# Zero-padded inverses in one place, weight splits one block ahead, and later reloads in a gated mix of linear attention and ReGLU

## The chip, the core and the metric

The kernel runs on one core of a Trainium2 chip. The metric is the device time of one execution in microseconds; the time before is the median of three runs. One further execution was taken by the hardware profiler, and all durations below come from it.

## The reference

```
g = sigmoid((x * gate_w).sum(-1))                       # x: 2048 x 576
q, k, v = split(x @ wqkv)                               # 32 heads of 18
phi(t) = concat(softmax(t @ w_phi), softmax(-t @ w_phi))  # per head
kv = sum_s phi(k)^T v ;  z = sum_s phi(k)
o = phi(q) kv / (phi(q) z + 1e-6)
a = o @ wo
b = (relu(x @ W_gate) * (x @ W_up)) @ W_down            # 576 -> 4608 -> 576
out = g * a + (1 - g) * b
```

All data are float32. The products are made in float32r with operands split into a high and a low part; the FFN's products go by a seven-product block scheme.

## The kernel before

**Stages.** The values of the first 512 tokens come first (L217 to L237): warm-up matmuls, then loads of a slice of x and of wv for each of five row groups k, split into high and low by ScalarE (ACT) and VectorE (DVE). A loop over tokens then makes keys, values, queries and the running sum kv. The out-projection goes over four blocks of 512 tokens, b = 0 to 3 (in the order BLOCKS). The FFN follows in two halves of 36 units, with a swap of operands and accumulators between the halves.

**The out-projection of one block.** `sums(b, ...)` (L556) multiplies the features ph with kvm, which gives numerators and denominators together. ACT copies the result to R and og (L560), and SP's queue gathers the denominators into dn (L562, L564). `invert(b)` takes the reciprocal on VectorE (L593), multiplies it with the gate (L594) and stores the product on SP into rows of kt (L595). `split_inverse(b)` splits it on POOL into rd, high and low (L603, L604); rd has two halves of 64 rows, one for odd and one for even b. `divide(b, k)` spreads the inverses of row group k over 128 rows by a matmul of rd with 0/1 columns (L616), multiplies R by them on VectorE (L618), and makes oh on ACT (L619) and ol on VectorE (L620). `first_out(k, mm)` (L633, block 0) or `project_out(b, m)` (L175, blocks 1 to 3) multiplies oh and ol with the output weights wo. `rows_out` copies the result o (L769 to L772) and stores it to att on SP (L773). `fetch` (L431) loads the features of a block from DRAM on POOL's queue, after `store_turned` (L392) has stored the last of them. Denominators and numerators share PSUM banks called kv, po and pw.

**What sets the order.** A scheduler orders ACT and VectorE; `in_order` keeps TensorE, SP and POOL in the order of the code, `after` and `behind` hold named instructions behind others. An instruction that waits holds all that stands behind it on its engine or queue.

**FFN.** `load_w(u)` loads the raw weights wr of unit u, and `unit(u)` splits them to wb, makes block sums of wr and splits these to ws (L846 to L870). The x operands xo are partly made in place from loaded rows: high part on ACT (L829, L830), low part on VectorE (L834, L814); `early()` does this for the operands 5 and 6. `step(u, j)` makes one of the seven products (L1098) of a unit, with ACT's copies g and u (L1259), VectorE's sums (L1378 to L1383, L1255) and down products (L1138, L1161) whose results are added to accumulators ac. wdr is the raw down weight of a unit, loaded on SP (L1031) and split to wd by ACT (L1061) and VectorE (L1064). At the swap `add_up` stores finished accumulators (L1182) and loads those of the second half from att (L1106); split weights of the first half come back from DRAM as wb and ws (L883, L884).

Of the kernel before, what the change touches and what calls it, by code (L numbers as in the profile page):

```python
# [14 lines left out]
DH = D // H  # L15
P = 128
# [67 lines left out]
def gated_mix_kernel(  # L84
# [126 lines left out]
    with tc.tile_pool(name="ps_v", bufs=1, space=PSUM) as ps_v:  # L211
# [7 lines left out]
        for k in range(5):  # L219
            w = raw.tile([P, TB + VW], F32, name="xwv", tag="raw")  # L220
            nc.sync.dma_start(w[:, :TB], xT[:, k, :TB])
            nc.sync.dma_start(w[:, TB:], wv[:, k])
# [367 lines left out]
    def invert(b):  # L590

        dn = DN.pop(b)
        nc.vector.reciprocal(dn, dn)  # L593
        tt(out=dn, in0=gT[:, BLOCKS[b] * P:(BLOCKS[b] + 1) * P], in1=dn, op=MULT)  # L594
        nc.sync.dma_start(kt_[2 * H * (b % 2):][:H, :TB], dn)  # L595

    def split_inverse(b):

        if not RD:
            RD.append(rb.tile([4 * H, TB], F32R, name="rd", bufs=1))  # L600
        i = 2 * H * (b % 2)
        d2, hi, lo = kt_[i:i + H, :TB], RD[0][i:i + H], RD[0][i + H:i + 2 * H]
        nc.gpsimd.tensor_copy(hi, d2)  # L603
        pt(out=lo, in0=d2, in1=hi.bitcast(F32), op=SUB)  # L604

    def divide(b, k):

        R = RW[b]
        n = P if k < 4 else 64
        if k == 4:  # L610
            pool = op_ if b else rb
            OW[b] = [pool.tile([P, j, TB], F32R, name=f"o{a}", bufs=2 if b else 1) for a, j in (("h", 5), ("l", 4))]
        oh, ol = OW[b]
        ps = kv_bank(1 - k % 2 if b > 1 or b == 1 and k < 2 else 0)
        half = slice(2 * H * (b % 2), 2 * H * (b % 2 + 1))
        nc.tensor.matmul(ps[:n], spread[half, k, :n], RD[0][half], start=True, stop=True)  # L616
        r = R[:n, k]
        tt(out=r, in0=ps[:n], in1=r, op=MULT)  # L618
        nc.scalar.activation(oh[:n, k], r, AF.Copy)  # L619
        tt(out=ol[:, k] if k < 4 else oh[64:, k], in0=r, in1=oh[:n, k].bitcast(F32), op=SUB)  # L620
# [43 lines left out]
    with in_order(tc, nc, nc.tensor, nc.sync, nc.gpsimd):  # L664
# [67 lines left out]
        divide(0, 3)  # L732
        two = pp.tile([P, 2, TB], F32, name="pw", tag="pp")
# [195 lines left out]
    with in_order(tc, nc, nc.tensor, nc.sync, nc.gpsimd):  # L929
        x0, x1, x2 = (operand_ahead(i) for i in range(3))  # L930
        fetch(BLOCKS[3], nc.gpsimd)
        load_operand(0, 0, nc.gpsimd)
        load_operand(0, 1, nc.gpsimd)
        first_out(2, range(5))
        halves = two[:, 0], two[:, 1]
        sums(2, (4, 5), halves)
        divide(0, 0)
        first_out(1, range(5))
        sums(2, (3, 2), halves)
# [5 lines left out]
        sums(2, (1, 0), halves)  # L945
        gather(2, 4)
        invert(2)
        gather(2, 3, 2, 1, 0)
        split_inverse(2)
        divide(1, 1)  # L950
        divide(1, 0)
        for m in range(5):
# [4 lines left out]
            if m == 2:  # L957
                gather(3, 4)
                invert(3)
                gather(3, 3, 2, 1, 0)  # L960
                split_inverse(3)
                whole(x0)
            if m > 0:
                divide(2, 5 - m)
            if m in (0, 1):
                root_rows(m + 2)
            if m == 4:
                divide(2, 0)
                whole(x1)
# [272 lines left out]

    def add_up():

        if PEND:
            done.extend(PEND.pop()())
        store(done)
        done.clear()
# [38 lines left out]
    def step(u, j):  # L1287
# [122 lines left out]
        if u == 0:  # L1410
            if j < 3:
                next(early, None)
            elif j < 5:
# [30 lines left out]
    later_half, early = second_half(), early()  # L1444
# [93 lines left out]
def _layout(A_x, A_wqkv, A_w_phi, A_wo, B_W_gate, B_W_up, B_W_down, gate_w):  # L1538
# [33 lines left out]
    spread = np.zeros((4, H, 5, P), np.float32)  # L1572
    for r in range(QK):
# [4 lines left out]
    for k in range(5):  # L1578
        for r in range(P):
            spread[:, wo_rows[k * P + r] // DH, k, r] = 1.0  # L1580
# [20 lines left out]
```

## Time and profile before

| | |
|---|---|
| median of three runs | 1607.55 us (1607.47 to 1607.68) |
| the profiled execution | 1607.92 us |
| its span, first to last instruction | 1605.9 us |
| mean granted TensorE clock | 0.997 |
| HBM read, written | 172.67 MB, 109.21 MB |
| TensorE matmuls | 7823 |

The span is what the trace shows; the execution's time holds some 2 us around it. A row of the timeline gives the start in us from the span's start, the duration in us, engine, line, operation, the tile written and read, shapes, and how often; a bracket gives the idle time of the engine just before the row and what ended it. A row of the waits names the engine that waited, the tile and line, what released it, the total, the number of times and the longest. PEld is TensorE's weight load, which runs beside its matmuls.

### The profile page before, as it was taken

Reading aid. Unit: us, or ns where it says so; the run is one execution under the profiler, and the core shown is the slowest. Engines: PE = TensorE matmul, PEld = TensorE weight load, DVE = VectorE, ACT = ScalarE, POOL = GpSimd, SP = SyncE. Lnnn points to the kernel's source line nnn. Section 1 sums busy time; section 2 is a strip of 40 time slices with the busy share of each in tenths; the row PEclk is TensorE's granted clock in tenths of the full one; section 3 lists DMA queues with packets and bytes.
Section 4 is the critical chain, followed back from the end, with each engine's and each line's share of the span. In section 5 each row is a group of like instructions: output and inputs, shape, how many; then the busy total and the mean of one; then the engine's idle time right before and its main releaser. Section 6 shows DMA issues by size and latency. Waiting matters only on the chain.

```text
span 1605.9 us, 20175 instructions
## 1 busy us (share of the span) xinstructions
PE 1580.5 (98%) x7823; PEld 1314.5 (82%) x7823; DVE 1192.4 (74%) x1864; ACT 559.9 (35%) x918; POOL 171.3 (11%) x234
## 2 busy tenths in 40 slices
PE   9999999899999999999999999999999999999998
PEld 9899995577888888888888887788888888888887
DVE  4997775477787877878777777677776777767777
ACT  4444335463332332333333234223223232232331
POOL 0125522100000000000000002111111111111110
PEclk9999999999999999999999999999999999999999
DMA  5373415569655565655554525634344343443432
GB/s 165 108 242 134 162 41 148 177 234 351 215 220 212 217 249 217 222 218 189 214 197 172 208 83 175 242 129 183 134 151 181 129 174 143 148 184 129 169 148 74
DMA packets 65370, 284.59 MB, mean 177 GB/s; under 512 B 6842, under 2 KB 17338, under 8 KB 56572
## 3 DMA queue, kind: packets, MB, share of 16 engines
q1 hardware_dynamic: 62828, 273.30, 46.8%
q0 software_dynamic: 1872, 8.97, 1.8%
q8 instruction: 61, 1.00, 0.2%
q10 hardware_dynamic: 576, 1.05, 0.2%
q14 instruction: 33, 0.27, 0.0%
HBM read 172.67 MB, written 109.21 MB: 176 GB/s over the span
## 4 chain that ended last, share of the span: by engine, by line
PE 91%; DMA 3%; DVE 3%; ACT 1%; issue 1%; POOL 0%; SPq 0%; ACTq 0%; DVEq 0%; POOLq 0%
PE cx L1098 28%; PE ca L1098 13%; PE pd L1138 12%; PE pd L1161 10%; PE cy L1098 7%; PE kv L175 4%; PE pq L175 3%; PE pk L175 3%; PE pm L1138 2%; PE pm L1161 2%; PE kv L417 1%; DMA dn<-R 1%; PE ptr L374 1%; PE pv L237 1%; DMA wdr<-wd 1%; PE pw L175 1%
## 5 line engine op out<-in xcount | busy, mean ns | idle before, releaser
L1205 ACT ACTIVATE hh<-g 128x512 fp32r<-128x512 f32 x195 | 120.1, 624 | 459.1 <-DVE g L1255 289.8
L1176 DVE TENSOR_TENSOR ac<-pd,ac 128x512 f32<-128x512 f32 x238 | 164.0, 689 | 145.9 <-PE pd L1161 145.7
L1098 PE MATMUL cx<-xo,wb 128*128 128x512 f32 x1008 | 250.9, 392 | 5.0 <-DVE u L1380 3.5
L1098 PE MATMUL cx<-xo,ws 128*128 128x512 f32 x1008 | 252.4, 390 | 3.0 <-ACT g L1259 2.8
L1098 PE MATMUL ca<-xo,ws 128*128 128x512 f32 x1008 | 252.0, 389 | 0.6 <-DMA ws<-wsd 0.6
L1098 PEld LDWEIGHTS cx<-xo,wb 128*128 128x128 f32 x1008 | 189.2, 189 | 47.1 <-DVE u L1380 4.4
L1098 PEld LDWEIGHTS cx<-xo,ws 128*128 128x128 f32 x1008 | 188.9, 188 | 43.8 <-ACT g L1259 4.7
L1098 PEld LDWEIGHTS ca<-xo,ws 128*128 128x128 f32 x1008 | 189.1, 188 | 40.3 <-issue 1.0
L1138 PE MATMUL pd<-hh,wd 128*128 128x512 f32 x576 | 200.7, 389 | 0.0
L1161 PE MATMUL pd<-hh,wd 128*128 128x512 f32 x476 | 185.2, 389 | 0.0
L1144 DVE TENSOR_TENSOR ac<-pd,ac 128x512 f32<-128x512 f32 x144 | 99.1, 688 | 106.6 <-PE pd L1138 103.1
L1210 DVE TENSOR_TENSOR hl<-g,hh 128x512 fp32r<-128x512 f32 x195 | 136.4, 699 | 1.9 <-ACT hh L1205 0.2
L1259 ACT ACTIVATE g<-cx 128x512 f32<-128x512 f32 x144 | 84.9, 590 | 128.1 <-PE cx L1098 128.0
L1138 PEld LDWEIGHTS pd<-hh,wd 128*128 128x128 f32 x576 | 108.1, 188 | 22.6
L1098 PE MATMUL cy<-xo,wb 128*128 128x512 f32 x504 | 125.9, 389 | 0.0
L1061 ACT ACTIVATE wd<-wdr 128x384 fp32r<-128x384 f32 (+1 forms) x106 | 62.3, 606 | 152.9 <-DMA wdr<-wd 152.9
L1138 PE MATMUL pd<-hl,wd 128*128 128x512 f32 x288 | 112.2, 389 | 1.0 <-ACT xo L830 1.0
L1098 PEld LDWEIGHTS cy<-xo,wb 128*128 128x128 f32 x504 | 94.6, 188 | 19.6
L1161 PEld LDWEIGHTS pd<-hh,wd 128*128 128x128 f32 x476 | 89.4, 188 | 18.5
L1161 PE MATMUL pd<-hl,wd 128*128 128x512 f32 x238 | 92.6, 389 | 0.0
L814 POOL TENSOR_TENSOR xo<-xr,xo 32x512 fp32r<-32x512 f32 x5 | 8.2, 1637 | 653.9 <-DVE xo L814 646.1
L1064 DVE TENSOR_TENSOR wd<-wdr,wd 128x384 fp32r<-128x384 f32 (+1 forms) x106 | 69.3, 669 | 5.5 <-ACT wd L1061 5.5
(250 smaller groups left out, 2564.9 us busy)
## 6 DMA issues: line engine op xcount, KB each, us to landing
wsd<-ws SPq DMA_DIRECT2D x34, 1280.0 KB
ws<-wsd SPq DMA_DIRECT2D x34, 1280.0 KB
wbd<-wb SPq DMA_DIRECT2D x34, 960.0 KB
wb<-wbd SPq DMA_DIRECT2D x34, 960.0 KB
wr<-wgu SPq DMA_DIRECT2D x36, 768.0 KB
wdr<-wd SPq DMA_DIRECT2D x36, 576.0 KB
eT<-et SPq DMA_DIRECT2D x10, 594.0 KB
xt<-xb SPq DMA_DIRECT2D x7, 768.0 KB
```

What stands on the lines that cost most here:

```text
L175: nc.tensor.matmul(ps, w, m, start=i == 0, stop=i == len(pairs) - 1)
L237: nc.tensor.matmul(pv[i][c], m, w_[:, k, cs], start=k == 0 and n == 0, stop=k == 4 and n == 1)
L1061: nc.scalar.activation(o[:, 0], a, AF.Copy)
L1064: tt(out=o[:, 1], in0=a, in1=o[:, 0].bitcast(F32), op=SUB)
L1098: nc.tensor.matmul(ps, w, v, start=first and m == 0, stop=m == len(pairs) - 1, skip_group_check=True)
L1138: nc.tensor.matmul(ps, w, v, start=k == 0 and (i < 2 or first), stop=k == len(mms) - 1 and (i < 2 or last), skip_group_check=True)
L1144: tt(out=a, in0=ps, in1=a, op=ADD)
L1161: mm = lambda ps, w, v, a, z: nc.tensor.matmul(ps, w, v, start=a, stop=z, skip_group_check=True)
L1176: tt(out=a, in0=ps, in1=a, op=ADD)
L1205: nc.scalar.activation(h, src, AF.Copy)
L1210: tt(out=l, in0=src, in1=h.bitcast(F32), op=SUB)
L1259: nc.scalar.activation(a, ps, AF.Copy)
```

## The change

It has five parts. The first two wv loads are issued from ACT's queue. The inverses of all blocks lie in one place: rd keeps 64 rows of data and 64 rows of zeros, and L616 multiplies all 128 rows. The out-projection is written in another order: where invert and split_inverse stand, which sums come ahead of first_out, and where POOL's loads stand. The first two units' weight splits come one block of the out-projection earlier, and early() moves from the first FFN unit to the last block. At the swap a reload comes three calls of add_up after its store, and load_rests one step earlier.

```diff
-            nc.sync.dma_start(w[:, TB:], wv[:, k])
+            (nc.scalar if k < 2 else nc.sync).dma_start(w[:, TB:], wv[:, k])
...
-        nc.sync.dma_start(kt_[2 * H * (b % 2):][:H, :TB], dn)
+        nc.sync.dma_start(kt_[:H, :TB], dn)
...
             RD.append(rb.tile([4 * H, TB], F32R, name="rd", bufs=1))
-        i = 2 * H * (b % 2)
-        d2, hi, lo = kt_[i:i + H, :TB], RD[0][i:i + H], RD[0][i + H:i + 2 * H]
+            nc.gpsimd.memset(RD[0][2 * H:].bitcast(F32), 0.0)
+        d2, hi, lo = kt_[:H, :TB], RD[0][:H], RD[0][H:2 * H]
...
-        half = slice(2 * H * (b % 2), 2 * H * (b % 2 + 1))
-        nc.tensor.matmul(ps[:n], spread[half, k, :n], RD[0][half], start=True, stop=True)
+        nc.tensor.matmul(ps, spread[:, k], RD[0], start=True, stop=True)
...
         divide(0, 3)
+        quotients = last_of(nc, nc.vector)
...
         divide(0, 2)
         gather(1, 4)
-        with after(tc, nc, nc.vector, last_of(nc, nc.vector)):
+        with after(tc, nc, nc.vector, quotients):
             invert(1)
         gather(1, 3, 2, 1, 0)
-        split_inverse(1)
...
         fetch(BLOCKS[3], nc.gpsimd)
-        load_operand(0, 0, nc.gpsimd)
-        load_operand(0, 1, nc.gpsimd)
-        first_out(2, range(5))
+        first_out(2, range(3))
         halves = two[:, 0], two[:, 1]
         sums(2, (4, 5), halves)
+        first_out(2, range(3, 5))
         divide(0, 0)
+        split_inverse(1)
+        sums(2, (3, 2), halves)
         first_out(1, range(5))
-        sums(2, (3, 2), halves)
+        sums(2, (1, 0), halves)
+        gather(2, 4)
         for m in range(5):
             first_out(0, (m,))
             rows_out(0, m, PW[m])
             if m in (0, 1, 3):
                 divide(1, (4, 3, None, 2)[m])
-        sums(2, (1, 0), halves)
-        gather(2, 4)
-        invert(2)
-        gather(2, 3, 2, 1, 0)
-        split_inverse(2)
+            if m == 3:
+                with after(tc, nc, nc.vector, last_of(nc, nc.vector)):
+                    invert(2)
+                gather(2, 3, 2, 1, 0)
         divide(1, 1)
         divide(1, 0)
+        split_inverse(2)
+        load_operand(0, 0, nc.gpsimd)
+        load_operand(0, 1, nc.gpsimd)
         for m in range(5):
             project_out(1, m)
...
             if m == 2:
                 gather(3, 4)
-                invert(3)
-                gather(3, 3, 2, 1, 0)
-                split_inverse(3)
                 whole(x0)
             if m > 0:
                 divide(2, 5 - m)
+            if m == 3:
+                with after(tc, nc, nc.vector, last_of(nc, nc.vector)):
+                    invert(3)
+                gather(3, 3, 2, 1, 0)
...
             if m == 4:
                 divide(2, 0)
+                split_inverse(3)
                 whole(x1)
         for m in range(5):
             project_out(2, m)
...
-        unit0, unit1 = unit(0), unit(1)
+            if m > 1:
+                with behind():
+                    if m == 2:
+                        unit0, unit1 = unit(0), unit(1)
+                        next(unit0)
+                    if m == 3:
+                        whole(unit0)
+                    if m == 4:
+                        next(unit1)
+        first = early()
         for m in range(5):
             project_out(3, m)
             with behind():
                 if m == 0:
-                    next(unit0)
-                if m == 1:
-                    whole(unit0)
-                if m == 2:
-                    next(unit1)
+                    whole(unit1)
                 if m == 3:
-                    whole(unit1)
+                    next(first)
+                if m == 4:
+                    next(first)
...
     def store(keys):
         for hf, i, m, t in keys:
             nc.sync.dma_start(out[rows(i, m, t, hf)], ACC.pop((hf, i, m, t)))
-            if hf == 0:
-                load_acc(1, i, m, t)
...
-            if i in (3, 4):
-                load_rests(1, (2, 3, 4) if i == 3 else (5, 6))
+            if i in (2, 3):
+                load_rests(1, (2, 3, 4) if i == 2 else (5, 6))
...
     def add_up():
 
+        if len(STORED) > 2:
+            for hf, i, m, t in STORED.pop(0):
+                if hf == 0:
+                    load_acc(1, i, m, t)
         if PEND:
             done.extend(PEND.pop()())
         store(done)
+        STORED.append(tuple(done))
         done.clear()
...
         if u == 0:
-            if j < 3:
-                next(early, None)
-            elif j < 5:
+            if 3 <= j < 5:
                 plain_down(0, (high, low)[j - 3])
```

The 0/1 columns are filled for the first 64 rows only. Three places show how the order moves; line numbers of the changed kernel are one lower here than those before, up to 17 higher in the FFN.

VectorE around the reciprocal of block 1 (L593). The ol rows are, from the top, those of block 0's row groups k = 3 and 2; before:

```order
L620 TENSOR_TENSOR ol<-R,oh 128x512
L618 TENSOR_TENSOR R<-kv_2978,R 128x512
L313 TENSOR_TENSOR gates<-gates 128x8
L314 TENSOR_SCALAR gates<-gates 128x8
L620 TENSOR_TENSOR ol<-R,oh 128x512
L593 RECIPROCAL dn<-dn 128x128
L594 TENSOR_TENSOR dn<-kt,dn 128x128
L618 TENSOR_TENSOR R<-kv_3032,R 128x512
```

And in the changed kernel:

```order
L619 TENSOR_TENSOR ol<-R,oh 128x512
L617 TENSOR_TENSOR R<-kv_2979,R 128x512
L593 RECIPROCAL dn<-dn 128x128
L619 TENSOR_TENSOR ol<-R,oh 128x512
L594 TENSOR_TENSOR dn<-kt,dn 128x128
L313 TENSOR_TENSOR gates<-gates 128x8
L314 TENSOR_SCALAR gates<-gates 128x8
L617 TENSOR_TENSOR R<-kv_3031,R 128x512
```

The reciprocal of block 1 moved from behind the ol of k = 2 to ahead of it.

TensorE at the end of first_out(2). kv_2967 before and kv_2968 after are the bank of output rows m = 3, kv_3094 and kv_3089 the divide of k = 0; L556 is sums(2, ...). Before:

```order
L633 MATMUL kv_2967<-oh,wo 128x512
L633 MATMUL kv_2967<-ol,wo 128x512
L633 MATMUL kv_2967<-oh,wo 128x512
L633 MATMUL pw<-oh,wo 128x512
L633 MATMUL pw<-ol,wo 128x512
L556 MATMUL po<-ph,kvm 64x512 x3
L616 MATMUL kv_3094<-rd,spread 128x512
L633 MATMUL pw<-oh,wo 128x512
```

And in the changed kernel:

```order
L556 MATMUL po<-ph,kvm 64x512 x3
L632 MATMUL kv_2968<-oh,wo 128x512
L632 MATMUL kv_2968<-ol,wo 128x512
L632 MATMUL kv_2968<-oh,wo 128x512
L632 MATMUL pw<-oh,wo 128x512
L632 MATMUL pw<-ol,wo 128x512
L615 MATMUL kv_3089<-rd,spread 128x512
L556 MATMUL po<-ph,kvm 64x512 x4
L632 MATMUL pw<-oh,wo 128x512
```

The first pair of sums moved ahead of the last two m of first_out(2), and the second pair (the x4 row) from behind first_out(1) to directly behind the divide of k = 0.

VectorE at the end of block 3. wb and ws are the split weights of unit 1, xo the in-place operands, o the last 64 output rows of block 3. Before:

```order
L867 TENSOR_TENSOR wr<-wr 128x384
L772 TENSOR_TENSOR o<-o,kv_3634 64x512
L868 TENSOR_TENSOR wr<-wr 128x384
L834 TENSOR_TENSOR xo<-xo 128x1024
L869 TENSOR_TENSOR wr<-wr 128x384
L814 TENSOR_TENSOR xo<-xr,xo 32x512
L870 TENSOR_TENSOR wr<-wr 128x384
```

And in the changed kernel:

```order
L869 TENSOR_TENSOR wr<-wr 128x384
L848 TENSOR_TENSOR ws<-wr,ws 128x4x256
L851 TENSOR_TENSOR ws<-wr,ws 32x4x128
L833 TENSOR_TENSOR xo<-xo 128x1024
L813 TENSOR_TENSOR xo<-xr,xo 32x512
L833 TENSOR_TENSOR xo<-xo 128x1024
L813 TENSOR_TENSOR xo<-xr,xo 32x512
L833 TENSOR_TENSOR xo<-xo 128x1024
L813 TENSOR_TENSOR xo<-xr,xo 32x512
L771 TENSOR_TENSOR o<-o,kv_3639 64x512
L833 TENSOR_TENSOR xo<-xo 128x1024
L813 TENSOR_TENSOR xo<-xr,xo 32x512
```

The last add of block 3 moved from between the block sums of unit 1 to behind both weight splits and three of the four operands.

More of the change, by code (lines that the diff above doesn't have):

```diff
@@ L1241, in gated_mix_kernel @@
     done = []
+    STORED = []
     def add_up():
+        if len(STORED) > 2:
+            for hf, i, m, t in STORED.pop(0):
+                if hf == 0:
+                    load_acc(1, i, m, t)
         if PEND:
@@ L1442, in step @@
                 load_operand(1, 1)
-    later_half, early = second_half(), early()
+    later_half = second_half()
     with in_order(tc, nc, nc.tensor, nc.vector, nc.scalar, nc.gpsimd, nc.sync):
@@ L1572, in _layout @@
     spread = np.zeros((4, H, 5, P), np.float32)
+    copies = spread[:2]
     for r in range(QK):
@@ L1579, in _layout @@
         for r in range(P):
-            spread[:, wo_rows[k * P + r] // DH, k, r] = 1.0
+            copies[:, wo_rows[k * P + r] // DH, k, r] = 1.0
     spread = spread.reshape(4 * H, 5, P)
```

## The prediction

> **What bounds the kernel now.** I read the page first, then TensorE's waits over the whole span, then busy time by stage. The page: TensorE is busy almost throughout.
>
> ```profile
> PE 1580.5 (98%) x7823; PEld 1314.5 (82%) x7823; DVE 1192.4 (74%) x1864; ACT 559.9 (35%) x918; POOL 171.3 (11%) x234
> ```
>
> 1605.9 - 1580.5 leaves 25.4 us of idle TensorE, so an edit that removes no matmul can win only a piece of that, plus time lost to a slow clock or to slow steps between matmuls. Where the idle time lies:
>
> ```profile
> PE cx L1098 <- DVE u L1380: 3.5, 2, 2.9
> PE cx L1098 <- ACT g L1259: 2.8, 3, 1.3
> PE kv L616 <- POOL rd L604: 2.6, 1, 2.6
> PE pv L217 <- DVE warm L215: 1.5, 1, 1.5
> PE cx L1098 <- DMA wb<-wbd: 1.4, 1, 1.4
> PE po L556 <- issue: 1.1, 1, 1.1
> ```
>
> The columns are total, times, longest. By stage (length; busy PE, PEld, DVE, ACT, POOL; granted clock):
>
> ```profile
> 340.00:367.00 27.00, 23.23 (x100) 18.25 (x99) 21.63 (x29) 16.52 (x22) 0.00 (x0) 1.00 0.83 295
> 367.00:405.00 38.00, 37.21 (x155) 30.27 (x156) 26.97 (x41) 14.37 (x20) 0.00 (x0) 0.96 0.88 331
> 405.00:960.00 555.00, 555.00 (x2450) 459.57 (x2449) 433.82 (x654) 188.05 (x253) 0.00 (x0) 1.00 0.55 203
> 960.00:1050.00 90.00, 85.00 (x370) 68.59 (x369) 62.04 (x91) 31.55 (x55) 15.04 (x19) 1.00 0.53 186
> ```
>
> From 405 to 960 there is nothing to win. The change touches the start, the out-projection (about 256 to 346), the FFN's start (340 to 372) and the swap of halves (960 to 1050). Two short stretches run at half clock:
>
> ```profile
> 303.60:307.00 3.40, 3.40 (x10) 2.58 (x11) 1.22 (x2) 1.11 (x2) 0.99 (x2) 0.50 0.68 243
> 368.45:371.85 3.40, 3.40 (x9) 2.65 (x8) 2.29 (x5) 2.31 (x3) 0.00 (x0) 0.50 1.03 433
> ```
>
> Each follows a TensorE wait of 2.6 or 2.9 us (the L616 and L1380 rows above), and 3.4 us at half clock do the work of 1.7. So a stall of that size really costs 1.7 us more. The Trainium skill, "TensorE: Matmul & The Clock Gate", Part 1, says the clock falls after an idle window of about 3.4 us in a free-running grid. The trace differs in one point: 2.6 us sufficed. By the page's rule taken strictly, only the longest wait below (4.2 us) could lose the clock at all, and the sum would be 1.7 us lower.
>
> **The start.** Lines L221/L222: the first two wv loads go to ACT's queue.
>
> ```profile
> 1.65 0.43 SPq L222 DMA_DIRECT2D xwv<-wv  x1
> ```
> ```profile
> 5.73 0.69 ACT L148 ACTIVATE wv_h<-xwv 128x588 fp32r<-128x588 f32 x1 [1.26 <-DMA xwv<-wv]
> ```
> ```profile
> 1.46 4.04 PE L217 MATMUL pv<-warm 128*128 128x294 f32 x15 [1.46 <-DVE warm L215]
> 6.48 1.84 PE L237 MATMUL pv<-wv_h,xh 128*128 128x294 f32 x6 [0.98 <-ACT wv_h L148]
> ```
>
> The first real matmul waits 0.98 us for ACT's split, which waits for wv's landing. The load can be issued up to about 0.9 us sooner, and the warm-up matmuls end at 1.46 + 4.04 = 5.50, so 0.98 is the most that this wait can give. ACT's own queue now holds two issues ahead of its first copy, but ACT idles 1.26 us there already. Taken: **-0.9** (ends 0 and -2.7: the upper end adds one grid step of 1.7, if TensorE without a gap gets its full clock sooner). The Trainium skill, "DMA: Bandwidth & Descriptors", section "Issuing engines are not separate DMA queues", says that another queue saves issue time alone; by it this would be one issue, 0.43 us.
>
> **Spread matmuls over 128 rows.** L616 runs 20 times.
>
> ```profile
> L616 PE MATMUL kv<-rd,spread x20: 388/498/684, 258.0 to 329.2; 64*128 64x512 f32 x16, 64*64 64x512 f32 x4
> ```
> ```profile
> 268.73 0.50 PE L616 MATMUL kv<-rd,spread 64*128 64x512 f32 x1
> 269.16 0.50 PE L633 MATMUL pw<-oh,wo 128*128 128x512 f32 x1
> 269.50 0.40 PE L633 MATMUL pw<-ol,wo 128*128 128x512 f32 x1
> 269.73 0.62 PE L633 MATMUL pw<-oh,wo 128*128 128x512 f32 x2
> ```
>
> The normal pace is the last step, 0.23. The steps 268.73 to 269.16 and on to 269.50 are 0.43 and 0.34, so a 64-row tile costs 0.31 beside its own time; 20 times 0.31 is 6.2. Many stand next to waits, or to L556's own 108*64 tiles, which stay. I count 8: **-2.5** (0 to -4). The zero rows are one POOL memset before the first reciprocals arrive, so nothing waits for it.
>
> **Block 0's third quotient behind block 1's reciprocal.** VectorE before:
>
> ```profile
> 265.60 0.69 DVE L620 TENSOR_TENSOR ol<-R,oh 128x512 fp32r<-128x512 f32 x1 [0.42 <-ACT oh L619]
> 271.96 0.95 DVE L593 RECIPROCAL dn<-dn 128x128 f32<-128x128 f32 x1 [5.66 <-DMA dn<-R]
> 272.95 0.29 DVE L594 TENSOR_TENSOR dn<-kt,dn 128x128 f32<-128x128 f32 x1
> ```
>
> That first row is ol for k=2; first_out(2) read it at 269.50. In the changed order the RECIPROCAL stands ahead of it, and it waits 5.66 us for the dn loads, which nothing in the change makes earlier (POOL's four ph fetches still run beside them). So ol starts where the dn product started, 272.95, ends at 273.64, and TensorE, which cannot pass it, goes on at about 273.7: **+4.2** (3.2 to 5). Behind it queue dn's product, the gates and R for k=1, which TensorE needs later only.
>
> **sums(2,(3,2)) behind divide(0,0).** Before, first_out(1) lay between.
>
> ```profile
> 276.52 1.51 DVE L620 TENSOR_TENSOR ol<-R,oh 128x512 fp32r<-128x512 f32 x1 [0.70 <-ACT oh L619]
> ```
> ```profile
> 278.07 0.59 ACT L560 ACTIVATE R<-po 64x512 f32<-64x512 f32 x1 [1.58 <-DVE ol L620]
> ```
> ```profile
> 278.71 1.94 PE L556 MATMUL po<-ph,kvm 108*64 108x512 f32 x8 [0.19 <-ACT R L560]
> ```
>
> The ol is k=0's. The copy that empties the second po half writes R of block 2, in block 0's old buffer, so it waits for the last ol of block 0, and the sums that reuse that half wait for the copy. The chain R (0.7), oh (0.7), ol (0.7 to 1.5), copy (0.6) starts one matmul after divide(0,0), and with 14 matmuls of 0.23 between, 0.19 us was left to wait. Now only the two matmuls of the first half (0.9) cover it: 2.9 to 3.7 less 0.9 is 2.0 to 2.8. Taken: **+2.5** (1.5 to 3.1).
>
> **What goes.** The 2.58 us at block 2's first divide:
>
> ```profile
> 303.56 0.68 PE L616 MATMUL kv<-rd,spread 64*64 64x512 f32 x1 [2.58 <-POOL rd L604]
> ```
>
> All of sums(2) now precedes first_out(0), and SP issues its dn loads before block 0's first four att stores, so that chain starts 14 matmuls (3.2 us) and four issues sooner: **-2.6** (0 to -2.6). What is late next is block 2's VectorE queue, below. POOL's fetch and store of the last block stood behind the split of block 1:
>
> ```profile
> 275.52 0.60 POOL L603 CAST rd<-kt 32x512 fp32r<-32x512 f32 x1 [14.66 <-DMA kt<-dn]
> 276.21 1.28 POOL L604 TENSOR_TENSOR rd<-kt,rd 32x512 fp32r<-32x512 f32 x1
> 277.44 0.58 POOL L392 DMA_DIRECT2D eT<-et  x1
> 278.01 1.65 POOL L431 DMA_DIRECT2D ph<-eT  x3
> ```
>
> They now go some microseconds sooner, so the 1.1 us "issue" idle at an L556, which I take for a late ph, may go: **-0.5** (0 to -1.1). They then lie beside kt<-dn of block 1, whose 2.3 us (end of L594 at 273.24 to 275.52) may become 5 to 8, under first_out(1) and two pairs of sums, which hide it. The xr loads now follow block 2's split; no wait on them stands in the list.
>
> **Clock.** The half-clock step after 303.56 goes (-1.7); the waits of 4.2 and 2.5 us bring one each (+3.4): **+1.7** (-1.7 to +3.4).
>
> **Blocks 2 and 3.**
>
> ```profile
> 297.89 0.95 DVE L593 RECIPROCAL dn<-dn 128x128 f32<-128x128 f32 x1 [6.49 <-DMA R<-og]
> ```
>
> RECIPROCAL and product of block 2 (0.95 + 0.29) now stand among the last two quotients of block 1, ahead of project_out(1,0), which cannot start without them: **+1.3** (0 to 2.5). Block 3's inversion waits for divide(2,2), its split for divide(2,0), since there is one place: 0.95 + 0.29 + 2.3 + 0.6 + 1.3 = 5.4 from reciprocal to divide(3,4), under project_out(1,4) and project_out(2,0), 14 matmuls or 3.2 us each: **+1.0** (0 to 3).
>
> **FFN start.** The weight splits come earlier, the in-place operands 5 and 6 later, on a VectorE that is busy 21.63 of 27 us.
>
> ```profile
> 343.29 0.96 DVE L849 TENSOR_TENSOR wb<-wr,wb 128x768 fp32r<-128x768 f32 x1 [3.50 <-ACT wb L846]
> ```
> ```profile
> 354.69 0.67 DVE L772 TENSOR_TENSOR o<-o,kv 64x512 f32<-64x512 f32 x1
> ```
> ```profile
> 362.56 1.23 DVE L834 TENSOR_TENSOR xo<-xo 128x1024 fp32r<-128x1024 f32 x1
> ```
> ```profile
> 360.72 1.26 ACT L1061 ACTIVATE wd<-wdr 128x1024 fp32r<-128x1024 f32 x2
> ```
>
> The L772 add now stands behind both weight splits and three operands, just ahead of the last operand, the 362.56 row: 7.9 us later in its queue. Its att store stands ahead of the first wdr load on SP, that load ahead of ACT's wd (6.0 us from the add to it), and VectorE's wd ahead of the u of L1380. Against it, the first split (343.29) has 3.5 us of idle VectorE in front of it and may start that much sooner, and TensorE comes 4.2 us later (the terms above added up). I take these to cancel, **0** (-4.6, the 2.9 us wait and its clock gone, to +3.7).
>
> **Swap.** Each reload stood behind its own store on SP:
>
> ```profile
> SPq L1106 <- DMA outT<-ac: 27.7, 8, 8.3
> ```
> ```profile
> 999.16 0.53 ACT L1061 ACTIVATE wd<-wdr 128x384 fp32r<-128x384 f32 x1 [14.84 <-DMA wdr<-wd]
> ```
>
> The weight loads queue behind these 27.7 us; ACT's g copies queue behind a wd split that waited 14.84 us, and TensorE behind g and wb. 960 to 1050 holds 5.0 us idle. I give back all but the in-place operand's 1.2: **-3.7** (0 to -4.7). The price is accumulators that come three steps later, of seven steps in a unit; no wait on them stands in the list.
>
> **The sum.** -0.9 - 2.5 + 4.2 + 2.5 - 2.6 - 0.5 + 1.7 + 1.3 + 1.0 + 0 - 3.7 = **+0.5**. The profiled execution took 1607.92, 0.37 above the median 1607.55; against that median the forecast is **1608.1**.
>
> **Rivals.**
> - *The early splits clear the FFN start.* If the add's place costs nothing, because the splits before it are through early, both the 2.9 us wait and its half clock go, -4.6: 1603.5. For it: the 3.5 us of head start; against it: the wdr chain. It decides if ACT's wd starts no later against TensorE than at 360.72, so if the add has lost no more than TensorE.
> - *The wdr chain takes the place of that wait (slower).* If the first wr load lands no earlier than before, nothing of the 7.9 us is won back by a head start; less the 4.2 by which TensorE itself comes later, it waits 3.7 us more than before: 1611.8. It decides once the add loses more than those 4.2 us. For it: the queue order; against it: the idle VectorE before 343.29.
> - *The swap doesn't do what it says.* If TensorE there waits for transfers that the DMA engines, not SP, hold up, -3.7 falls away: 1611.8. Against it: DMA is at 0.53 in that stage.
>
> **How the numbers follow.** Forecast 0.40, cleared FFN start 0.27, wdr chain 0.20, swap without gain 0.13. One measurement can tell about 0.2% or 3.2 us from no change, 1604.3 to 1610.8. Faster: 0.22 of the second case and 0.07 of the first, 0.29. Slower: 0.17 of the third, 0.10 of the fourth and 0.07 of the first, 0.34. Same: 0.37. The range runs from the second case with a further 1.7 for the clock at the start, 1601.8, to the third with one more half-clock step, 1613.5: 1602 to 1614.
>
> **What would show it.** Right: VectorE's k=2 ol of block 0 at about 273 behind RECIPROCAL, and TensorE waiting about 4 us for it; an L556 waiting 2 to 3 us for ACT's R; no wait on rd; half clock behind both; ACT's wd waits in the swap short. Wrong: dn landing before 268, full clock through 270 to 290, or a wait on ac in the swap.

## The result and the profile after

The changed kernel took 1611.57 us (median of 10 runs, 1609.97 to 1614.04) beside 1607.62 (10 runs, 1606.62 to 1609.89): a ratio of **1.0022** with a 95% interval of 1.0012 to 1.0031. The forecast was 1608.1 with a range of 1602 to 1614. The time is in the range, and the sign that was left open came out as slower, by 3.5 us by the ratio and 3.95 by the medians, a little over the 3.2 us (0.2%) named there. The profiled execution has a span of 1609.9 us, 4.0 more than before.

The page after: TensorE's busy time fell by 1.9 us while the span grew by 4.0.

```profile
PE 1578.6 (98%) x7823; PEld 1315.6 (82%) x7823; DVE 1191.9 (74%) x1864; ACT 560.0 (35%) x918; POOL 169.9 (11%) x235
```

TensorE's waits after, the longest first (total, times, longest):

```profile
PE cx L1110 <- DVE u L1397: 5.8, 2, 5.2
PE pw L632 <- DVE ol L619: 4.3, 2, 4.0
PE po L556 <- ACT R L560: 2.8, 1, 2.8
PE pd L1150 <- DVE hl L1220: 1.6, 1, 1.6
...
PE pw L175 <- DVE ol L619: 1.5, 2, 1.2
PE kv L175 <- ACT oh L618: 1.3, 1, 1.3
PE kv L615 <- POOL rd L604: 1.1, 1, 1.1
```

The 2.6 us wait on block 2's rd, the "issue" wait and the waits on wb and ws of the swap are gone; the rd row of 1.1 is block 3's. In their place stand the two waits that were forecast for block 0 (ol L619, R L560), and the wait on u at the FFN's start has grown from 2.9 to 5.2. The same by stage (the stages lie some 8 us later than before):

```profile
340.00:373.00 33.00, 28.73 (x126) 23.10 (x124) 21.88 (x29) 17.85 (x24) 0.00 (x0) 1.00 0.69 241
373.00:410.00 37.00, 34.98 (x141) 28.39 (x142) 26.30 (x41) 12.02 (x16) 0.00 (x0) 0.91 0.98 374
410.00:968.00 558.00, 558.00 (x2464) 462.03 (x2463) 435.56 (x656) 190.08 (x256) 0.00 (x0) 1.00 0.55 204
968.00:1058.00 90.00, 88.45 (x390) 72.72 (x389) 66.59 (x99) 34.35 (x61) 14.41 (x19) 1.00 0.57 197
```

The swap's 90 us hold 1.55 us of idle TensorE instead of 5.0. The clock column of the second row says 0.91 where it said 0.96. Windows around the stretches at half clock, five grid steps (of 3.41 us, worked out below) in place of two:

```profile
271.00:274.38 3.38, 2.90 (x7) 2.33 (x8) 2.16 (x6) 0.63 (x1) 1.11 (x2) 0.50 0.88 245
281.25:284.60 3.35, 3.35 (x8) 0.68 (x8) 0.00 (x0) 0.00 (x0) 1.86 (x2) 0.50 0.36 77
329.05:332.40 3.35, 3.35 (x10) 2.57 (x9) 3.20 (x5) 1.23 (x2) 0.00 (x0) 0.50 0.39 117
373.40:380.20 6.80, 5.77 (x14) 4.56 (x15) 4.63 (x9) 2.31 (x3) 0.00 (x0) 0.50 1.02 429
```

Half of the busy time in these rows is what the clock cost: 7.7 us, beside 3.4 before.

Where TensorE stood against before, by the first and last starts of single lines:

| the same work | before | after | shift |
|---|---|---|---|
| first L556 (block 0's sums) | 243.4 | 241.5 | -1.9 |
| first product of the FFN | 353.0 | 358.7 | +5.7 |
| 201st product into cx, well behind the FFN's start | 471.7 | 480.0 | +8.3 |
| last down product, L1161/L1173 | 1587.8 | 1591.5 | +3.7 |

So the out-projection lost 7.6 us, and its rows come near that sum: waits 13.6 after and 6.3 before (+7.3), three half-clock steps with 9.6 us of work instead of one with 3.4 (+3.1), and about 3 us won by the padding (e5 below), together +7.4. The FFN's start lost 2.6 more, and the swap won 4.6 (e4 below says 4.7 by the time).

**The first long wait**, on VectorE and then TensorE:

```profile
269.93 0.95 DVE L593 RECIPROCAL dn<-dn 128x128 f32<-128x128 f32 x1 [6.83 <-DMA dn<-R]
270.80 0.63 DVE L619 TENSOR_TENSOR ol<-R,oh 128x512 fp32r<-128x512 f32 x1
```
```profile
267.08 0.40 PE L632 MATMUL pw<-oh,wo 128*128 128x512 f32 x1
271.48 0.80 PE L632 MATMUL pw<-ol,wo 128*128 128x512 f32 x1 [4.00 <-DVE ol L619]
```

VectorE did nothing for 6.83 us with ol's operands ready behind the reciprocal; TensorE had the first product of the same row group done at 267.08 and could not go on.

**The second**, right behind the divide of k = 0:

```profile
281.17 1.11 PE L556 MATMUL po<-ph,kvm 108*64 108x512 f32 x2 [2.79 <-ACT R L560]
```

**The third**, at the FFN's start, goes over four engines (VectorE, SP, ACT, VectorE, TensorE):

```profile
365.20 0.68 DVE L771 TENSOR_TENSOR o<-o,kv 64x512 f32<-64x512 f32 x1
...
372.35 1.43 DVE L1076 TENSOR_TENSOR wd<-wdr,wd 128x1024 fp32r<-128x1024 f32 x2 [3.90 <-ACT wd L1073]
373.69 0.68 DVE L1397 TENSOR_TENSOR u<-cx,u 128x512 f32<-128x512 f32 x1
```
```profile
365.90 0.45 SPq L772 DMA_DIRECT2D att<-o  x1
366.45 0.54 SPq L1043 DMA_DIRECT2D wdr<-wd  x1
```
```profile
371.26 1.06 ACT L1073 ACTIVATE wd<-wdr 128x1024 fp32r<-128x1024 f32 x1 [6.19 <-DMA wdr<-wd]
```
```profile
374.43 0.80 PE L1110 MATMUL cx<-xo,wb 128*128 128x512 f32 x1 [5.22 <-DVE u L1397]
```

The add at 365.20 releases the store, the store lets wdr be issued at 366.45, ACT's wd waits 6.19 us for it, VectorE 3.90 us for ACT, and u comes behind. Against the add's 354.69 before that is 10.5 us later, against TensorE's own shift of 5.7. Not all of the 4.8 between them became waiting, since before ACT's wd was through at 361.98 and VectorE, busy without a gap, took it up 3.15 us later:

```profile
365.13 1.41 DVE L1064 TENSOR_TENSOR wd<-wdr,wd 128x1024 fp32r<-128x1024 f32 x2
```

So u itself came 7.2 us later (366.47 before, 373.69 after), 1.5 more than TensorE. The longer half clock behind it (5.8 us of work instead of 3.4) adds 1.2.

### The profile page after: what moved, and what is told of

The parts are those of the page before. It is cut to its first block, busy times and chain, and to the rows that moved or that the text cites. A ratio compares the mean times of both kernels' runs of the same rounds, so it can differ in the third digit from the quotient of the medians.

```text
span 1609.9 us, 20177 instructions
## 1 busy us (share of the span) xinstructions
PE 1578.6 (98%) x7823; PEld 1315.6 (82%) x7823; DVE 1191.9 (74%) x1864; ACT 560.0 (35%) x918; POOL 169.9 (11%) x235
## 4 chain that ended last, share of the span: by engine, by line
PE 92%; DVE 4%; DMA 2%; ACT 1%; issue 1%; POOL 0%; SPq 0%; DVEq 0%; POOLq 0%; ACTq 0%
PE cx L1110 28%; PE ca L1110 14%; PE pd L1150 12%; PE pd L1173 10%; PE cy L1110 7%; PE kv L175 4%; PE pq L175 3%; PE pk L175 3%; PE pm L1150 2%; PE pm L1173 2%; PE kv L417 1%; PE ptr L374 1%; PE po L556 1%; PE pw L175 1%; PE pv L237 1%; DMA dn<-R 1%
## 5 line engine op out<-in xcount | busy, mean ns | idle before, releaser
L1173 PE MATMUL pd<-hh,wd 128*128 128x512 f32 x476 | 185.2, 389 | 0.0
L1173 PEld LDWEIGHTS pd<-hh,wd 128*128 128x128 f32 x476 | 89.3, 188 | 18.6
L1173 PE MATMUL pd<-hl,wd 128*128 128x512 f32 x238 | 92.6, 389 | 0.0
```

The lines of the kernel that those rows point to most:

```text
L1173: mm = lambda ps, w, v, a, z: nc.tensor.matmul(ps, w, v, start=a, stop=z, skip_group_check=True)
```

## The experiments

Ratios are to the kernel before on the same chip, with 95% intervals; the changed kernel's is 1.0022. The runs lie on several chips, so a difference between two kernels other than the kernel before is taken from their two ratios. One per mille is 1.6 us. "The changed kernel" is the base of e1 to e3, e5, e8 and e9, "the kernel before" that of the others.

### e1: the reciprocal of block 1 back

```diff
-        with after(tc, nc, nc.vector, quotients):
+        with after(tc, nc, nc.vector, last_of(nc, nc.vector)):
             invert(1)
```

> The changed kernel with one thing undone: the inversion of block 1 is held behind the third divide's VectorE work again, so the ol of k=2 stands ahead of RECIPROCAL. My theory (a queue order on VectorE, price 4.2 us of wait plus one half-clock step of 1.7): TensorE's 4.0 us wait on ol L619 near 271 goes, 1611.6 falls to 1605.7 to 1607.4; the wait on ACT's R of about 2.8 us stays. Rival (the wait only moves: TensorE arrives sooner and meets the R copy or block 2's rd instead): the R wait grows to about 7 us and the time stays at 1610 to 1612.

Measured: 1606.51 us, ratio 0.9985 (0.9975 to 0.9995), so 6.0 us below the changed kernel. The wait on ol L619 fell to 0.3, and the next one stayed as it was:

```profile
PE po L556 <- ACT R L560: 2.9, 1, 2.9
```

The theory holds: it was the queue order, and the wait did not move to the R copy. What the trace does not show is the half-clock step in the price. The profiled execution has five such steps as well, at other places, and reached the FFN 4.05 us sooner than the changed kernel, the wait alone. Its granted clock was 0.995, as in seven others (0.994 or 0.995); four of the twelve executions had 0.996 or 0.997 and took 1602.8 to 1604.4.

### e2: the second pair of sums back

```diff
         split_inverse(1)
-        sums(2, (3, 2), halves)
         first_out(1, range(5))
-        sums(2, (1, 0), halves)
-        gather(2, 4)
+        sums(2, (3, 2), halves)
...
                 divide(1, (4, 3, None, 2)[m])
+            if m == 1:
+                sums(2, (1, 0), halves)
+                gather(2, 4)
```

> The changed kernel with the second pair of sums of block 2 behind first_out(1) again, and the third pair inside first_out(0). My theory (ACT's R copy waits for the last ol of block 0, and first_out(1) is what covered it): the 2.8 us wait on ACT R goes, with one half-clock step, 1611.6 falls to 1607 to 1608.7. Rival (the sums were moved because block 2's reciprocal is otherwise late): TensorE waits 2 to 3 us on rd or on VectorE at block 2's first divide instead, and the time stays within 1 us of 1611.6.

Measured: 1607.27, ratio 0.9999 (0.9991 to 1.0008): 3.7 us below the changed kernel. No wait on R stands in TensorE's list, and the waits on rd in block 2 and 3 stayed at 1.1. Its profiled execution has four half-clock steps instead of five. The theory holds; the rival, block 2 being late, did not show.

### e3: wdr on POOL's queue

```diff
-    def load_down(g):
+    def load_down(g, queue=nc.sync):
...
-            nc.sync.dma_start(WDR[g], wd[units[2 * g][1] // 2])
+            queue.dma_start(WDR[g], wd[units[2 * g][1] // 2])
...
-        load_down(0)
+        load_down(0, nc.gpsimd)
```

> The changed kernel with the first down-weight load (wdr) on POOL's queue, which is idle there, instead of behind the last att store on SP. My theory (the late add holds the att store, the store holds wdr, wdr holds wd and so u): TensorE's wait of 5.2 us on u L1397 falls below 1.5 and the two half-clock steps behind it go, 1611.6 falls by 5 to 8, to 1603.6 to 1606.6. Rival (VectorE's own work, busy from 343.9 to 368.4, is what makes u late): the wait falls by at most 1 us, and the time stays above 1610.

Measured: 1608.22, ratio 1.0003 (0.9995 to 1.0012): 3.1 us below the changed kernel, between the two ranges and so in neither. TensorE's waits on u and g in the stretch from 340 to 400:

```profile
PE cx L1110 <- DVE u L1397: 3.0, 2, 1.7
PE cx L1110 <- ACT g L1276: 1.8, 2, 1.3
```

The wait of 5.2 us is gone, so wdr behind the late add was what held u; VectorE, as busy as before, was not. What is left of that wait, 1.26 us, is VectorE's: it had no gap from 355 until u. But what else SP has behind that store is still late: on ACT the weight split of the next unit waits 2.27 us for a weight store, and ACT's next g, behind it in the queue, is the one that TensorE waits 1.3 us for:

```profile
372.56 1.17 ACT L845 ACTIVATE wb<-wr 128x1152 fp32r<-128x1152 f32 x1 [2.27 <-DMA wbd<-wb]
```

The mechanism was right, the gain too high. From the FFN's first product to the 201st into cx this execution took 117.3 us beside 121.2, 4.0 less; 2.1 of them were lost again at the swap, where a step at 985.8 ran at granted clock 0.50 and none did in the changed kernel's.

### e4: the swap alone

```diff
-            if hf == 0:
-                load_acc(1, i, m, t)
...
+        if len(STORED) > 2:
+            for hf, i, m, t in STORED.pop(0):
+                if hf == 0:
+                    load_acc(1, i, m, t)
```

The rests one step earlier belong to it as well.

> The kernel before with the swap's part of the change alone: reloads three calls after their stores, and the rests one step earlier. My theory (SP's queue held the weight loads behind store-and-reload pairs): TensorE's 5.0 us of idle time between 960 and 1050 falls to about 1, 1607.6 falls to 1602.9 to 1604. Rival (the part only pays because the out-projection's delay shifted the swap against its transfers): the gain is under 1.5 us.

Measured: 1602.77, ratio 0.9971 (0.9959 to 0.9982): 4.7 us below the kernel before. Of SP's 27.7 us behind L1106 and TensorE's waits between 955 and 1050 this is left:

```profile
SPq L1106 <- DMA outT<-ac: 4.6, 2, 3.2
```
```profile
PE pd L1138 <- ACT u L1264: 1.5, 1, 1.5
```

The time is just below the range. The theory holds for SP's queue, and the part pays without the rest of the change: the first wb reload of the swap is issued at 994.31 instead of 1000.13.

### e5: without the zeros

```diff
-            nc.gpsimd.memset(RD[0][2 * H:].bitcast(F32), 0.0)
...
-        nc.tensor.matmul(ps, spread[:, k], RD[0], start=True, stop=True)
+        nc.tensor.matmul(ps[:n], spread[:2 * H, k, :n], RD[0][:2 * H], start=True, stop=True)
```

> The changed kernel with its spread matmuls over the 64 data rows alone again (still one place, no zeros), nothing else undone. My theory (each isolated 64-row tile costs about 0.3 us of drain at its neighbours): the step from such a matmul to the next grows from 0.23 to 0.43 and the one behind it to 0.34, together 1.5 to 3 us where no wait hides it, so 1613 to 1614.6. Rival (all of these matmuls stand beside waits, which swallow it): within 0.7 us of the changed kernel, 1611.6.

Measured: 1614.62, ratio 1.0041 (1.0028 to 1.0054), 3.0 us above the changed kernel. The padding is worth about 3 us, at the upper end of what was expected; the two intervals overlap by a little (1.0028 to 1.0031). The traces say the same: without TensorE's waits and what half clock cost, the out-projection takes 101.9 us here, 98.8 in the changed kernel and 101.6 before.

### e6: the start alone

```diff
-            nc.sync.dma_start(w[:, TB:], wv[:, k])
+            (nc.scalar if k < 2 else nc.sync).dma_start(w[:, TB:], wv[:, k])
```

> The kernel before with the start's part alone: the first two wv loads on ACT's queue. My theory (the first matmul comes 0.5 to 0.7 us sooner, and the gap behind the warm-up matmuls shrinks, so that the full clock comes a grid step sooner in most executions): first real matmul at about 5.9 instead of 6.48, the time 0.5 to 2 us below 1607.5, so 1605.5 to 1607. Rival (chance of the clock grid alone; the earlier load gives nothing that lasts, since the token loop is VectorE's): within 0.3 us of 1607.5.

Measured: 1608.09, ratio 0.9997 (0.9987 to 1.0007), no difference. The first real matmul started at 5.88 instead of 6.48. This execution stood 2.0 us ahead of before at 252, and then waited longer where a transfer ends the wait, near 256 and 303:

```profile
PE kv L616 <- POOL rd L604: 6.0, 2, 5.0
```

Whether the start's gain was real and given back, or chance, this run alone cannot say; e11 tests it.

### e7: the early splits alone

The edit is that of the change: the units' splits at project_out(2), early() at the end of project_out(3).

> The kernel before with the early weight splits and the late in-place operands alone, and its out-projection as before. My theory (the last add falls behind splits and operands, and wdr on SP behind it): TensorE's wait on u near 367 grows from 2.9 to 5 or 7 us, its wait on ACT's g of 1.1 goes, one more half-clock step may come: 1608.5 to 1612. Rival (the early splits pay when the out-projection is not late): that wait falls below 2, and the time is 1603 to 1606.

Measured: 1610.38, ratio 1.0016 (1.0007 to 1.0025): 2.6 us above the kernel before. From 340 to 400:

```profile
PE cx L1105 <- DVE u L1387: 6.9, 2, 5.8
```

The theory holds: with the out-projection as it was, the early splits still cost, by the place of the last add.

### e8: three mends of the changed kernel

e1 and e2 together, and the last add on POOL:

```diff
-            tt(out=o, in0=o, in1=ps[:64], op=ADD)
+            if b < 3:
+                tt(out=o, in0=o, in1=ps[:64], op=ADD)
+            else:
+                o2 = tb_.tile([n, TB], F32, name="o", tag="tb")
+                nc.scalar.activation(o2, ps[:64], AF.Copy)
+                pt(out=o, in0=o, in1=o2, op=ADD)
```

> The changed kernel with three mends: block 1's inversion behind the third divide again, the second pair of sums of block 2 behind first_out(1) again, and the last add of block 3 on POOL (ACT copies both halves) instead of VectorE, so that the last att store and wdr leave SP sooner; start, padding, early splits and swap stay. If the three waits are separate, their gains add: 6.0 and 3.8 us by the two single runs and 3 to 6 for the add, so 1596 to 1599. Rival (they share half-clock steps, and block 2's or 3's VectorE queue takes over): 1600 to 1603.

Measured: 1602.40, ratio 0.9960 (0.9948 to 0.9973). That is the rival's range: the gains did not add. The wait on u fell to 1.4, but a wait of 4.05 us stands at block 1's first divide. POOL tells why:

```profile
269.31 1.70 POOL L431 DMA_DIRECT2D ph<-eT  x3
273.22 0.56 POOL L431 DMA_DIRECT2D ph<-eT  x1 [2.21 <-DMA eT<-et]
281.01 0.60 POOL L603 CAST rd<-kt 32x512 fp32r<-32x512 f32 x1 [7.24 <-DMA kt<-dn]
```

The store of block 1's inverses, 64 KB and issued at 270.88, lands at 281, with four loads of 594 KB issued from 269 on beside it. In the changed kernel it landed as late, at 281.91, but TensorE stood at other waits until then.

### e9: and the feature loads later

```diff
-        fetch(BLOCKS[3], nc.gpsimd)
         first_out(2, range(3))
...
         split_inverse(1)
+        fetch(BLOCKS[3], nc.gpsimd)
```

> e8_three_undone with POOL's four feature loads of the last block behind the split of block 1 again. In e8 a new wait of 4.2 us stands at block 1's first divide, on rd. My theory (the early feature loads share the DMA engines with the small store of block 1's inverses to kt, which then lands late): that wait falls below 1 us and the time from 1602.4 to 1597 to 1600. Rival (block 1's reciprocal itself is late, or the late feature loads stop the sums of block 3): a wait of 3 us or more on rd, or on ph, and 1601 to 1603.

Measured: 1598.96, ratio 0.9945 (0.9930 to 0.9960), 2.4 us below e8 by the ratios and 3.4 by the medians; the two intervals overlap. POOL now:

```profile
273.47 0.60 POOL L603 CAST rd<-kt 32x512 fp32r<-32x512 f32 x1 [3.92 <-PE kv L615]
274.16 1.29 POOL L604 TENSOR_TENSOR rd<-kt,rd 32x512 fp32r<-32x512 f32 x1
275.40 2.21 POOL L431 DMA_DIRECT2D ph<-eT  x4
```

The split waits for TensorE's last reading of rd, no longer for a transfer: the store, issued at 270.45, had landed by 273.47. So the theory holds for the wait, which this pair of traces shows; the gain in time is less sure. Part of it went into a longer wait at project_out(1,0), 2.6 us on ACT's oh instead of 1.2.

### e10: block 2's chain alone

```diff
-        load_operand(0, 0, nc.gpsimd)
-        load_operand(0, 1, nc.gpsimd)
         first_out(2, range(5))
...
             first_out(0, (m,))
+            if m == 0:
+                sums(2, (1, 0), halves)
+                gather(2, 4)
             rows_out(0, m, PW[m])
...
-        sums(2, (1, 0), halves)
-        gather(2, 4)
-        invert(2)
-        gather(2, 3, 2, 1, 0)
-        split_inverse(2)
         divide(1, 1)
         divide(1, 0)
+        with after(tc, nc, nc.vector, last_of(nc, nc.vector)):
+            invert(2)
+        gather(2, 3, 2, 1, 0)
+        split_inverse(2)
+        load_operand(0, 0, nc.gpsimd)
+        load_operand(0, 1, nc.gpsimd)
```

> The kernel before with block 2's chain alone moved: its last pair of sums behind the first of block 0's five first_out(0), ahead of the att stores, its inversion behind block 1's last quotients, and the xr loads behind its split. My theory (block 2's denominators wait behind stores and loads on the DMA engines; sent ahead of them they land in time): the 2.6 us wait on rd near 303 and its half-clock step go, 1607.5 to 1608.5 falls by 3.5 to 6. Rival (VectorE's queue of block 1 and 2 makes a new wait of 2 us or more at project_out(1,0)): 1606 or more.

Measured: 1600.89, ratio 0.9959 (0.9946 to 0.9973), 6.6 us below the kernel before, a little more than expected. No wait on rd and none over 0.7 us is left between 255 and 340, and after the start the clock was full throughout, the stretch behind the 2.9 us wait on u included. In the profiled execution the out-projection itself, from its first sums to the FFN, gained 4.6; it was reached 1.5 sooner because of an early full clock, and 1.1 more were won at the FFN's start, where no half clock followed u, so neither is the chain's.

### e11: the start on top of it

The edit is e6's, put into e10.

> e10_block2_chain with the first two wv loads on ACT's queue as well. Alone (e6) the start gained 2.0 us up to 252 and had lost them by 358, at the rd wait near 303, which grew from 2.6 to over 5. My theory (that wait ends with a transfer and not with TensorE's work, so it takes back what comes early): without it the start's gain lasts, 1 to 2 us below e10. Rival (the start's gain is the clock grid's chance): within 0.6 us of e10.

Measured: 1601.49, ratio 0.9962 (0.9948 to 0.9976), 0.5 us above e10 by the ratios and not different from it. The rival holds. What the clock does at the start shows in the matmuls of one stretch from 6.60 to 10.00. Before, e10 (wv on SP's queue) and e12 (wv on ACT's):

```profile
6.60:10.00 3.40, 3.40 (x14) 3.40 (x15) 3.32 (x5) 2.71 (x5) 0.00 (x0) 1.00 0.95 346
```
```profile
6.60:10.00 3.40, 3.40 (x27) 3.40 (x27) 3.19 (x6) 3.00 (x6) 0.00 (x0) 1.00 1.06 368
```
```profile
6.60:10.00 3.40, 3.40 (x16) 3.40 (x15) 2.73 (x5) 2.39 (x5) 0.00 (x0) 1.00 0.92 291
```

27 matmuls are the full pace, 14 to 16 about half (the clock column has no record yet and reads 1.00). The full pace came at 10.0 before and at 4.5 in e10, both with the loads where they were, and at 10.0 in e12 and 4.5 in e11, both with the change: the place of the loads does not decide it. That it hangs on the phase of the clock's grid in each execution is the reading that remains; no run sets that phase. Nor is the first matmul's start the change's alone: with the loads on SP it came at 6.48, 6.34, 5.89 and 5.75 (before, e10, e4, e7), with the first two on ACT at 5.84 to 6.47 in ten traces. The changed kernel's profile, 1.9 us ahead at 243, had its full pace early, at 4.7.

### e12: the kernel before with what gained

e10, the start, the swap (e4), the early splits and the add on POOL (e8).

> The kernel before with the parts that gained: the start, block 2's chain as in e10, the early weight splits with the last add of block 3 on POOL, and the swap. rd keeps its two halves and no zeros, block 0 and block 1 keep their order. If the parts add: 4.5 for the swap, 3.5 to 6 for the chain, 1 to 2 for the start and 3 to 4 for the FFN start, 1593 to 1597. Rival (the early splits do not pay with an early out-projection, or shared half-clock steps): 1597 to 1600.

Measured: **1596.24**, ratio 0.9926 (0.9911 to 0.9942), below both kernels and in the expected range, though the start's 1 to 2 us cannot be part of it by e11. Its FFN start gained 2.5 us by the profiles, from the first product to the 201st into cx; no run has the early splits and the add on POOL alone. The longest wait left:

```profile
PE cx L1112 <- DVE u L1399: 2.8, 2, 1.7
```

Its rd has no zeros; no run has the padding beside this order.

## Why the prediction held, and where it did not, point by point

- **ol behind the reciprocal, +4.2**: right; 4.00 us measured. e1 shows the cause, and a price of 6.0 by the time; that the 2.0 over the wait are a half-clock step, its trace does not show.
- **Sums behind the divide, +2.5**: right; 2.79 measured, e2 3.7 with its clock step.
- **The wait on rd, -2.6, and the idle "issue", -0.5**: right, both gone (the second 1.1 instead of 0.5); e10 shows that sending block 2's denominators sooner is enough. The sign "no wait on rd" did not hold for block 3, see there.
- **Block 2's queue, +1.3**: right; TensorE waited 1.3 us for ACT's oh.
- **Block 3, +1.0**: too small. Its waits between 290 and 340 (1.5 on ol, 1.1 on rd, 0.9 on R, 0.5 on oh) come to 4.0 beside 1.5 before, so +2.5. The 5.4 us from reciprocal to divide(3,4) were laid under two projections. But the reciprocal started at 322.50, when project_out(1,4) was through, so project_out(2,0) alone covered 6.15 us (to 328.65), and it stood itself for 1.2 us on an ol behind that reciprocal.
- **Clock, +1.7**: mis-sized. The out-projection, for which the term was worked out, paid 3.1 more than before, 1.4 over the forecast; the whole span paid 7.7 instead of 3.4, and the other 1.2 lie at the FFN's start. Each stall was priced by itself. Block 3's waits, none over 1.2 us, fell into one grid step, and that step was followed by half clock too:

```profile
267.57:270.98 3.41, 0.00 (x0) 0.00 (x0) 1.05 (x2) 0.56 (x2) 1.66 (x3) 1.00 0.87 306
277.81:281.22 3.41, 0.61 (x5) 0.18 (x3) 1.39 (x2) 1.22 (x2) 0.00 (x0) 1.00 0.96 245
325.60:329.01 3.41, 1.59 (x5) 0.80 (x6) 2.25 (x2) 2.42 (x3) 1.86 (x2) 1.00 0.24 66
...
373.38:376.79 3.41, 2.36 (x6) 1.90 (x7) 2.29 (x5) 0.63 (x1) 0.00 (x0) 0.50 1.02 429
298.29:301.70 3.41, 2.12 (x8) 1.13 (x10) 2.43 (x5) 1.31 (x3) 0.46 (x1) 1.00 0.10 31
```

The grid comes from the clock records of this trace: half clock began at 270.98, 281.22, 329.01 and 373.38, and the distances, 10.24, 47.79 and 44.37 us, are 3, 14 and 13 times 3.413; the full clock at the start began at 4.74, 78 such steps before 270.98. Of the steps at full clock, those with 0, 0.61 and 1.59 us of TensorE work were followed by half clock, the one with 2.12 was not. So it is the idle time of a step that counts here, not the longest wait. Over all kept traces the border is not sharp: behind the first 20 us, every step at full clock with less than 1.5 us of work was followed by half clock and none with 2.0 or more, and between them both occurred. A step already at half clock is another case: behind the one with 2.36 us it stayed at half, behind the one from 270.98 with 2.9 it did not. The Trainium skill, "TensorE: Matmul & The Clock Gate", Part 1, speaks of an idle window: read as a wholly idle one, the strict reading in the prediction, it is refuted by the 1.59 us of work and by the 0.61 us in the step before 281.2; its free-running grid agrees with the 78 steps above.
- **FFN start, 0**: wrong by 2.6, about 1.5 of idle time and 1.2 of clock, and the largest miss. The chain from the add over wdr to u was right, and e3 shows it: the add lost 10.5 us, TensorE 5.7, and of the 4.8 between them all but the 3.15 us that wd had lain ready before became waiting. The step that failed is the head start of 3.5, set against the add beside TensorE's own delay:

```profile
343.88 0.96 DVE L848 TENSOR_TENSOR wb<-wr,wb 128x768 fp32r<-128x768 f32 x1 [3.46 <-ACT wb L845]
```

The splits' first row came not sooner than 343.29 but 0.6 later, because the out-projection's own loss was already in it; in e7, without that loss, it came at 337.86, 5.4 sooner. A delay of the out-projection moves the splits along with TensorE (from e7 to the changed kernel by 6.0 and 6.5), so it could not be counted for TensorE alone. The queue was longer as well: from the first split to the add 21.3 us, 9.9 more than before instead of 7.9. e7 shows the cost without the late out-projection, 2.6, so the early splits cost as much either way.
- **Start, -0.9**: not borne out. The first real matmul came at 5.96 instead of 6.48, but it came as early in runs without this part, and e11 finds nothing of it in the time. What the Trainium skill says of this ("DMA: Bandwidth & Descriptors", section "Issuing engines are not separate DMA queues"), that only the issue time is saved, agrees with e11's ratio beside e10's.
- **Padding, -2.5**: right, 3.0 by e5. **Swap, -3.7**: right, 4.7 by e4, but one sign of its mechanism did not show. ACT's waits for wdr in the swap are hardly shorter; before and after:

```profile
ACT wd L1061 <- DMA wdr<-wd: 28.3, 2, 14.8
```
```profile
ACT wd L1073 <- DMA wdr<-wd: 21.3, 2, 13.1
```

What went are TensorE's waits on g, wb and ws. Loads that leave SP's queue sooner explain that, but which of them was decisive for g stays open.

The sum was +0.5. Measured term by term in the order of the prediction's sum it is -1.9 - 3.0 + 4.0 + 2.8 - 2.6 - 1.1 + 3.1 + 1.3 + 2.5 + 2.6 - 4.6 = +3.1, beside +3.7 by the last down product; the -1.9 is the two executions' full clock at the start, which is chance. Too little was put on FFN start (2.6), block 3 (1.5) and clock (1.4), a little too little on swap and padding on the other side. The two costs of block 0 were foreseen with cause and size. That the time lies in the range owes something to a range of 12 us and to misses of opposite sign. The rival of the wdr chain describes the FFN start better than the main line did, and its threshold (the add loses more than TensorE) was passed; that its 1611.8 nearly meets the 1611.57 measured is luck, since it put 3.7 us on the FFN's start, and block 3 and the clock made up the rest. The rival of a cleared FFN start fell by its own condition, and the one of a swap without gain by e4.

## What to carry to other kernels

An engine's queue is a promise in order: before an instruction that waits for a transfer is moved up, read what stands behind it and who needs that, VectorE's ol here and SP's wdr there. A change of many parts can hold gains and losses of the same size, and parts tested alone (swap, block 2's chain, padding) show which to keep: the best version took gains and left the two reorderings that cost. When one wait is taken away, look at the transfer that it hid, as e8 and e9 show.

## What was not expected of the hardware

One kernel's executions spread by several microseconds (the kernel before from 1605.3 to 1612.2), and the granted clock goes with it: in the runs beside the experiments, those of the kernel before at a mean clock of 0.999 took 1605.5 to 1607.2, those at 0.995 took 1608.2 to 1612.2. The traces, one execution of each kernel, show two places where the clock can differ. The pace at the start doubles at 4.5 us in one execution (e10) and at 10.0 in another (e12). A wait of 2.9 us on u was followed by half clock in the kernel before, where it left one grid step with 1.24 us of work, and not in e10, where it fell across two steps with 2.17 and 1.72. A single profile's clock losses are therefore partly its phase, and an effect of a few tenths of a per cent needs many runs.
